# Matrix comparisons moved from the attention heads into the prologues

## The chip, the cores and the metric

The kernel runs on one core of one Trainium2 chip. Its engines are named as in the profile: PE (TensorE, matrix products), PEld (loading the weights of a product), DVE (VectorE), ACT (ScalarE), POOL (GpSimd) and SP (SyncE, which issues all of this kernel's transfers from one queue, in order). The metric is the device time of one execution in microseconds, the median of several runs.

## The reference

Two attention layers and two Fourier layers alternate, each with a layer norm in front and a residual sum behind; sequence 2048, width 640, 32 heads of 20, a sliding window of 256. All data are float32.

```python
def _A_ref(x, wqkv, wo):
    qkv = transpose((x @ wqkv).reshape(B, S, 3, H, Dh), 2, 0, 3, 1, 4)
    q, k, v = qkv[0], qkv[1], qkv[2]
    scores = jnp.einsum("bhqd,bhkd->bhqk", q, k) * (Dh ** -0.5)
    mask = (idx[:, None] - idx[None, :] >= 0) & (idx[:, None] - idx[None, :] < W)
    p = _softmax(jnp.where(mask[None, None], scores, -1e9), axis=-1)
    o = jnp.einsum("bhqk,bhkd->bhqd", p, v)
    return transpose(o, 0, 2, 1, 3).reshape(B, S, D) @ wo

def _B_ref(x, dft_seq_re, dft_seq_im, dft_hid_re, dft_hid_im):
    a = jnp.einsum("bsd,ed->bse", x, dft_hid_re)
    b = jnp.einsum("bsd,ed->bse", x, dft_hid_im)
    return jnp.einsum("ts,bse->bte", dft_seq_re, a) - jnp.einsum("ts,bse->bte", dft_seq_im, b)

x = x + _A_ref(_layernorm(x), A_wqkv, A_wo)
x = x + _B_ref(_layernorm(x), ...)
x = x + _A_ref(_layernorm(x), A_wqkv, A_wo)
x = x + _B_ref(_layernorm(x), ...)
```

The Fourier matrices are inputs like any other. The kernel computes the Fourier layers in a folded form that holds only if these matrices have the symmetries of a Fourier transform, and it tests that on the chip: this is what the "comparisons" or "checks" are. If a test fails, a general version of the whole network runs behind.

## The kernel before

**The layers.** Each attention layer has a prologue (`before_heads`), the heads (`heads`) and an end (`after_heads`); the Fourier layers follow (`fourier`). The program is written out in order: each engine executes its instructions in the order in which the Python code emits them, and waits for semaphores where data or buffers are not ready. In the heads small planners choose PSUM banks and post work to later steps (`post`, `tick`, `job`), but this too is settled when the program is built.

**The prologue.** It normalizes 16 tiles of 128 rows (`prep`: load, statistics on DVE, a power on POOL at L310, the normalization on DVE at L315, transposes on PE at L362, splitting into high and low parts on ACT at L243 and DVE at L249). Between these stand 16 value tiles (`value(t)`, t from 0 to 15, 30 matrix products each at L256) and, for each group of four tiles, two pieces of queries and keys (`pieces`, `piece`). A value tile fills two PSUM banks out of three (role "v": 5, 6, 7); ACT evicts the first (L478) and DVE the second (L480). After each second tile SP stores the pair to DRAM (`v_d<-pt`, L482). `packed` loads queries and keys back in the arrangement that the heads use (`kp<-qk_d`, `qp<-qk_d`, L639).

**The heads.** 128 steps in each attention, one 128-row block of a quad of heads each. Per step: four score products (L676) with a mask addition and row maximum on DVE each (L681), two pairs of transposed score products (L704), their exponentials on ACT (L714), the window's corners cleared on POOL (L720, L724), and the products with the values (L739). Beside them runs the projection of the remaining queries and keys (L274); its results pass through ACT (L589) and POOL (L597, L228), and its weights come as chunks that are split on ACT (L236) and DVE (L228, `wc<-x,wc`, two parts a chunk).

**A check.** `check(buf)` loads a block of four or eight parts of a matrix that should be equal or opposite (L1490, 214 or 228 KB, `rr<-kr` or the like), subtracts or adds the first part from or to the others (L1497, one or two instructions; on POOL in the attentions), squares and sums the result (L1501 on ACT, which also reads the sum). After each eighth check DVE adds up eight sums (L1506). There are 180 checks. In the prologue `check()` inside `before_heads` takes one of five small buffers in turn (`ou` and `rr`), and `check_step` holds a check's arithmetic back until two more have been begun, so a check's POOL and ACT instructions stand three checks behind its transfer in program order. In the heads `check_in_heads` issues a check at certain steps, `IN_HEADS` times over the first `CHECKED` = 81 steps (every six or seven steps), into the next `rr` buffer, with its three parts posted 6, 7 and 9 slots later. The Fourier layers take 14 buffers and work off the rest.

Before the change the first attention makes 16 checks in its prologue (6 in the pieces, 10 beside value tiles 4 to 13) and 12 in its heads; the second makes 22 (8 in the pieces, 14 beside value tiles 0 to 13) and 12. That is 62 of the 180.

Of the kernel before, what the change touches and what calls it, by code (L numbers as in the profile page):

```python
# [50 lines left out]
PRODUCTS = [(n, c) for n in ("ce", "co", "so", "se") for c in range(3)]  # L51
SIGMA, WIDE = 513, 57
SCALED, MARGIN = 2.0 ** 40, 2.0 ** 12
IN_HEADS, CHECKED = 12, 81

CHUNKS = ((0, 16, 0, 8), (0, 16, 8, 16), (16, 24, 0, 16), (24, 32, 0, 16), (0, 32, 16, 20))

# [16 lines left out]
class Net:  # L74
    def __init__(self, nc, tc, ctx, a, ok=None):
        self.nc, self.tc, self.a = nc, tc, a
        self.general = ok is None
        const = ctx.enter_context(tc.tile_pool(name="const", bufs=1))
        self.ln = ctx.enter_context(tc.tile_pool(name="ln", bufs=5))
        self.slots = ctx.enter_context(tc.tile_pool(name="slots", bufs=1))  # L80
        psum = ctx.enter_context(tc.tile_pool(name="psum", bufs=1, space=PSUM))
        self.work = ctx.enter_context(tc.tile_pool(name="work", bufs=2))
        dram = ctx.enter_context(tc.tile_pool(name="dram", bufs=1, space=DRAM))

        self.banks = psum.tile([P, 8, 512], F32, name="banks")

        def fixed(name, cols, dt):
            return const.tile([P, cols], dt, name=name)

        self.ident = fixed("ident", P, F32)  # L90
        nc.sync.dma_start(self.ident, a["ident"])
        self.flip = fixed("flip", P, F32)
        nc.sync.dma_start(self.flip, a["flip"])
        self.mask = fixed("mask", 384, BF16)
        self.ones = const.tile([1, 128], F32, name="ones")
        nc.vector.memset(self.ones, 1.0)
        self.half = fixed("half", 1, F32)
        nc.vector.memset(self.half, -0.5)
        self.big = [None] * 4
        self.qp, self.kp = [None] * 2, [None] * 2  # L100

        self.qk = dram.tile([2, 2 * D, S], F32, name="qk_d")
        self.vd = dram.tile([NQ, P, NB, 96], F32, name="v_d")
        self.od = dram.tile([H, 32, S], F32, name="o_d")
        self.rd = dram.tile([NSB, H, 512], F32, name="r_d")
        self.xs = [dram.tile([S, D], F32, name=f"x_d{i}") for i in range(3)]
        self.turn = {}
        self.xn = {}
        self.first = True
        self.slot = None  # L110
        self.posted = {}
        self.lanes = {n: deque() for n in ("act", "dve", "pool")}
        self.heavy = []
        self.left = 0
        self.tmp = None
        self.held = []
        self.bank_of = {}
        self.seen = fixed("seen", 2, F32)
        self.checks = deque() if self.general else deque(self.all_checks())
        self.stages = deque()  # L120
        self.n_checks = 0
        if not self.general:
            self.ok = ok
            self.ring = fixed("ring", 16, F32)
            self.part = fixed("part", len(self.checks) // 8 + 1, F32)
            self.norms = fixed("norms", 4, F32)
# [283 lines left out]
    def before_heads(self, xsrc):  # L410
        nc, a = self.nc, self.a
        self.proj = self.project()
        first = self.first
        vst = [t.rearrange("p (q t c) -> p q t c", t=2, c=96) for t in self.pt[:2]]
        for v in self.pt[:2]:
            (nc.vector if first else nc.gpsimd).memset(v, 1.0)
        for t in range(6):
            self.prep_load(xsrc, t)
            if first and 2 < t < 5:
                self.load_chunk(t - 3)  # L420
        if first:
            mask = self.raw()[:, :384]
            nc.sync.dma_start(mask, a["mask"])
        self.prep_stats(0)
        self.prep_stats(1)
        self.prep_norm(0)
        state = [0, 6]
        here = self.ou + self.rr
        wv = self.wv

        def check():
            here.append(here.pop(0))
            self.check_step(here[0][:, :8 * WIDE])

        def prep():
            r = state[0]
            if state[1] < r + 5:
                self.prep_load(xsrc, state[1])
                state[1] += 1
            self.prep_stats(r + 2)  # L440
            self.prep_norm(r + 1)
            if r == 10 or r == 11:
                self.prep_norm(r + 2)
            if r == 11:
                self.prep_stats(14)
                self.prep_stats(15)
                self.prep_norm(14)
            if r == 12:
                self.prep_norm(15)
            self.prep_turn(r)  # L450
            state[0] += 1

        def pieces(sb):
            for c in range(2):
                if sb == 0:
                    prep()
                self.piece(c, sb, "q")
                if c or sb > 1 or not first:
                    check()
                if sb and state[0] < 4 * sb + 8:  # L460
                    prep()

        def value(t):
            v, xt = vst[t // 2 % 2], self.xnt(t // 4)
            rs = slice((t % 4) * P, (t % 4 + 1) * P)
            ps = []
            for hf in range(2):
                p = self.bank("v", 320)
                cs = slice(hf * 320, (hf + 1) * 320)
                self.all3(p, [((xt[:, 0, k, rs], xt[:, 1, k, rs]), (wv[k][0][:, cs], wv[k][1][:, cs]))  # L470
                              for k in range(KC)])
                ps.append(p)
            prep()
            for hf in range(2):
                dst = v[:, 4 * hf:4 * hf + 4, t % 2, 0:84].rearrange("p q (h c) -> p q h c", c=21)[:, :, :, 1:21]
                src = ps[hf].rearrange("p (q h c) -> p q h c", q=4, h=4)
                if hf == 0:
                    nc.scalar.activation(dst, src, AF.Copy)  # L478
                else:
                    nc.vector.tensor_copy(dst, src)  # L480
            if t % 2:
                nc.sync.dma_start(self.vd[:, :, t - 1:t + 1, :].rearrange("q p t c -> p q (t c)"),  # L482
                                  v.rearrange("p q t c -> p q (t c)"))
            if 3 < t < 14 or t < 4 and not first:
                check()
            elif t > 13:
                for _ in range(t - 13):
                    self.check_step()

        def values(sb):  # L490
            for i in range(4):
                value(4 * sb + i)

        def packed(sb):
            for f in self.pack(0, sb):
                f()

        self.split_w(4)
        prep()
        self.split_w(6)  # L500
        prep()
        self.split_w(3 * KC)
        for t in range(4):
            if t in (1, 2):
                self.cut_chunk(t - 1)
            value(t)
        if first:
            nc.gpsimd.tensor_copy(self.mask, mask)
        while state[1] < NB:
            self.prep_load(xsrc, state[1])  # L510
            state[1] += 1
        pieces(0)
        pieces(1)
        self.take_qk("kp", 0)
        self.ones_rows(0)
        packed(0)
        packed(1)
        values(1)
        pieces(2)
        self.load_chunk(2)  # L520
        packed(2)
        values(2)
        pieces(3)
        self.cut_chunk(2)
        self.load_chunk(3)
        packed(3)
        values(3)
        while self.stages:
            self.check_step()
        self.pt += [self.slot_tile(f"pt{i}", 3 * 512, F32) for i in (2, 3)]  # L530
        for name in ("kp", "qp"):
            self.take_qk(name, 1)
        self.ones_rows(1)
# [1178 lines left out]
```

## Time and profile before

| what | value |
|---|---|
| median of three runs | 1366.66 us (1366.66, 1367.58, 1358.52) |
| the profiled execution's own time | 1368.62 us |
| its span on the core | 1366.9 us |
| first prologue | about 0 to 124 us |
| first attention's heads and end | about 124 to 600 us |
| first Fourier layer | about 600 to 688 us |
| second prologue | about 688 to 797 us |
| second attention's heads and end | about 797 to 1260 us |
| second Fourier layer | about 1260 to 1367 us |

The table's stages are read from when each line first and last runs. A profile row begins with the line of the kernel (L681), the engine, the operation and the tiles written and read; busy time adds up an engine's instructions, and the idle time of a group is the time that its engine stood still just before it, with the event that ended it. The clock column is the share of TensorE's full clock. Busy time on PE is modelled from starts of matrix products, so a PE that is called busy is not one at its peak.

### The profile page before, as it was taken

How to read it: one execution, taken by the hardware profiler on the slowest of the kernel's cores; microseconds unless marked ns; L12 is line 12 of the kernel's file. 1: busy time of each engine (PE TensorE's matmuls, PEld its weight loads, DVE VectorE, ACT ScalarE, POOL GpSimd, SP SyncE). 2: the span in 40 equal slices, each digit the busy share in tenths (PEclk: the TensorE clock that was granted, in tenths of full speed). 3: DMA queues.
4: the chain of work that ended last, by engine and by line, in shares of the span. 5: the costliest groups of instructions: out<-in, count | busy, mean ns of one | idle time of the engine just before them, and what ended most of it. 6: DMA issues, size and time to landing. Idle time of an engine off the chain costs nothing.

```text
span 1366.9 us, 37415 instructions
## 1 busy us (share of the span) xinstructions
PE 1293.2 (95%) x13350; PEld 995.8 (73%) x13350; DVE 973.2 (71%) x3117; ACT 761.4 (56%) x1651; POOL 729.3 (53%) x1508
## 2 busy tenths in 40 slices
PE   6999999999998999999999999999999988989996
PEld 6899777777776777753689997777777767778344
DVE  6723788888887774776866247888888877657674
ACT  3232378776876565446323225777777755744463
POOL 4221677776777673310334237787777875733043
PEclk9999999999999999999999999999999999999999
DMA  5675567776668864527536755676777688571565
GB/s 196 209 221 175 183 196 202 211 199 188 205 208 239 225 201 141 164 77 225 193 110 203 228 163 184 195 201 197 213 201 223 211 245 198 169 213 56 169 209 205
DMA packets 174297, 261.49 MB, mean 191 GB/s; under 512 B 36306, under 2 KB 85586, under 8 KB 174100
## 3 DMA queue, kind: packets, MB, share of 16 engines
q1 hardware_dynamic: 174100, 259.00, 62.8%
q8 instruction: 108, 1.77, 0.6%
q14 instruction: 89, 0.73, 0.2%
HBM read 175.42 MB, written 82.31 MB: 189 GB/s over the span
## 4 chain that ended last, share of the span: by engine, by line
PE 40%; DMA 3%; DVE 3%; issue 2%; ACT 2%; POOL 1%; SPq 1%; ACTq 0%; POOLq 0%; DVEq 0%
PE banks L274 10%; PE banks L256 8%; PE banks L739 5%; PE banks L704 4%; PE banks L676 4%; PE banks L1301 3%; PE banks L1409 3%; DMA big<-x_d 1%; PE banks L1425 1%; DVE banks L681 1%; ACT pt L714 1%; DMA qp<-qk_d 1%; DMA qp<-mt 1%; PE banks L362 1%; POOL rs L1156 0%
## 5 line engine op out<-in xcount | busy, mean ns | idle before, releaser
L681 DVE CUSTOM_DVE_ANT_0 banks<-banks,mask 128x384 f32<-128x384 f32 (+2 forms) x1024 | 527.0, 556 | 115.4 <-PE banks L676 97.3
L714 ACT ACTIVATE pt<-banks 128x768 f32<-128x768 f32 (+2 forms) x512 | 394.9, 773 | 163.3 <-PE banks L704 80.7
L720 POOL TENSOR_SCALAR_AFFINE_SELECT pt<-pt 128x256 f32<-128x256 f32 x512 | 219.7, 429 | 198.4 <-ACT pt L714 173.4
L274 PE MATMUL banks<-big,wc 64*128 64x512 f32 x1920 | 272.9, 394 | 0.4 <-DVE pt L480 0.4
L704 PE MATMUL banks<-qp,kp 61*128 61x384 f32 (+2 forms) x1024 | 209.8, 380 | 25.3 <-DVE mc L681 19.7
L676 PE MATMUL banks<-kp,qp 60*128 60x384 f32 (+2 forms) x1024 | 209.3, 352 | 8.5 <-DVE mc L681 5.1
L739 PE MATMUL banks<-pt,vq 128*32 128x128 f32 x5760 | 211.4, 278 | 0.9 <-ACT pt L714 0.8
L274 PEld LDWEIGHTS banks<-big,wc 64*128 64x128 f32 x1920 | 187.7, 186 | 22.0 <-ACT x L589 1.5
L724 POOL TENSOR_SCALAR_AFFINE_SELECT pt<-pt 128x256 f32<-128x256 f32 x448 | 186.5, 416 | 0.0
L739 PEld LDWEIGHTS banks<-pt,vq 128*32 128x32 f32 x5760 | 142.4, 110 | 49.3 <-issue 35.7
L704 PEld LDWEIGHTS banks<-qp,kp 61*128 61x128 f32 x1024 | 108.1, 185 | 88.9 <-DVE mc L681 66.5
L676 PEld LDWEIGHTS banks<-kp,qp 60*128 60x128 f32 x1024 | 124.5, 187 | 34.7 <-DVE mc L681 20.5
L681 DVE DVE_READ_ACCUMULATOR2_ANT mc<- 128x1 f32 x1024 | 143.7, 140 | 0.0
L748 ACT ACTIVATE ou<-banks 128x128 f32<-128x128 f32 (+2 forms) x288 | 73.7, 268 | 62.0 <-PE banks L739 55.3
L256 PE MATMUL banks<-qp,big 128*128 128x320 f32 x576 | 99.6, 318 | 1.0 <-POOL qp L382 1.0
L228 POOL TENSOR_TENSOR c<-x,c 128x256 fp32r<-128x256 f32 x128 | 94.3, 744 | 0.0
L256 PEld LDWEIGHTS banks<-qp,big 128*128 128x128 f32 x576 | 89.5, 194 | 1.6 <-POOL qp L382 1.4
L256 PE MATMUL banks<-qp,kp 128*128 128x320 f32 x384 | 82.2, 346 | 6.5 <-ACT big L1121 4.2
L274 PE MATMUL banks<-big,big 64*128 64x320 f32 x912 | 81.3, 314 | 0.2 <-ACT mt L692 0.2
L256 PEld LDWEIGHTS banks<-qp,kp 128*128 128x128 f32 x384 | 61.0, 188 | 19.9 <-ACT big L1121 6.2
L274 PEld LDWEIGHTS banks<-big,big 64*128 64x128 f32 x912 | 74.1, 191 | 0.4 <-ACT mt L692 0.4
L1497 POOL TENSOR_TENSOR rr<-rr 128x171 f32<-128x171 f32 (+3 forms) x76 | 48.5, 648 | 47.2 <-DMA rr<-hr 17.9
(170 smaller groups left out, 1787.2 us busy)
## 6 DMA issues: line engine op xcount, KB each, us to landing
qk_d<-c SPq DMA_DIRECT2D x80, 512.0 KB
kp<-qk_d SPq DMA_DIRECT2D x384, 80.0 KB
qp<-qk_d SPq DMA_DIRECT2D x384, 80.0 KB
o_d<-ou SPq DMA_DIRECT2D x64, 256.0 KB
v_d<-pt SPq DMA_DIRECT2D x16, 768.0 KB
vq<-v_d SPq DMA_DIRECT2D x64, 192.0 KB
kp<-ki SPq DMA_DIRECT2D x44, 228.0 KB
big<-x SPq DMA_DIRECT2D x26, 320.0 KB
```

What stands on the lines that cost most here:

```text
L228: eng.tensor_tensor(out=lo[..., c], in0=src[..., c], in1=hi[..., c].bitcast(F32), op=OP.subtract)
L256: self.nc.tensor.matmul(p, x, y, start=n == 0, stop=n == last)
L274: self.nc.tensor.matmul(ps[a], x[r], y[r], start=half + i == 0, stop=half == 1 and i == n - 1, skip_group_check=True)
L676: nc.tensor.matmul(p, qp[quad % 2][b:b + 60, z, qb * P:(qb + 1) * P], kp[quad % 2][b:b + 60, z, k0 * P:(qb + 1) * P], start=True, stop=True)
L681: nc.vector.tensor_tensor_reduce(out=p, in0=p, in1=self.mask[:, 384 - n * P:], scale=1.0, scalar=NEG, op0=OP.add, op1=OP.max, accum_out=mc ...
L704: nc.tensor.matmul(self.banks[:, banks[e], :n * P], kp[quad % 2][b:b + 61, z, kb * P:(kb + 1) * P], qp[quad % 2][b:b + 61, z, kb * P:(kb + ...
L714: nc.scalar.activation(pt[quad, kb][:, 2 * z:2 * z + 2, :n * P], self.banks[:, b0:b1 + 1, :n * P], AF.Exp, scale=SCALE)
L720: nc.gpsimd.affine_select(out=t[:, :, 0:P], in_=t[:, :, 0:P], pattern=[[0, 2], [1, P]], compare_op=OP.is_ge, fill=0.0, base=0, channel_mul ...
L724: nc.gpsimd.affine_select(out=t[:, :, 256:384], in_=t[:, :, 256:384], pattern=[[0, 2], [-1, P]], compare_op=OP.is_gt, fill=0.0, base=0, ch ...
L739: nc.tensor.matmul(self.banks[32 * h:32 * h + 32, bank, :P], vq[:, 96 * (kb % 4) + 21 * h:96 * (kb % 4) + 21 * h + 32], t[:, h, (qb - kb) ...
L748: nc.scalar.activation(ou[:, dst], self.banks[:, bank, src], AF.Copy)
L1497: eng.tensor_tensor(out=t[:, lo:hi], in0=t[:, lo:hi], in1=base.broadcast_to([P, hi - lo, w]), op=op)
```

## The change

No check is made in the heads any more (`IN_HEADS` is 0). In the prologues every value tile from 0 to 13 makes a check, in the first attention too, where tiles 0 to 3 had none; from tile 4 on it makes two. So the first prologue makes 30 checks and the second 32, 62 together as before; the first Fourier layer begins with the 31st check and not with the 29th. The counter `checked`, which the heads used to set, now gets a start value. The order of checks, their arithmetic and the two drains beside tiles 14 and 15 are the same. Since one line is added above it and another further below, line numbers of the changed kernel are 1 or 2 higher.

```diff
-IN_HEADS, CHECKED = 12, 81
+IN_HEADS, CHECKED = 0, 81
...
         self.n_checks = 0
+        self.checked = 0
...
-            if 3 < t < 14 or t < 4 and not first:
-                check()
+            if t < 14:
+                for _ in range(1 + (3 < t)):
+                    check()
             elif t > 13:
                 for _ in range(t - 13):
                     self.check_step()
```

## The prediction

> **What bounds the kernel now.** I read the page first, then the busy time by stage, then what the matrix engine (PE) waited for in the stages that the change touches, then one stretch of the timeline in which it stood still. The page's first lines:
>
> ```profile
> span 1366.9 us, 37415 instructions
> ...
> PE 1293.2 (95%) x13350; PEld 995.8 (73%) x13350; DVE 973.2 (71%) x3117; ACT 761.4 (56%) x1651; POOL 729.3 (53%) x1508
> ```
>
> Busy time of each engine in single stretches: two of the first prologue, one of the first attention's heads, then the same two stages of the second attention (columns: stretch, its length, the five busy times with instruction counts, clock, DMA share, GB/s):
>
> ```profile
> core 0: us, PE busy (x) PEld busy (x) DVE busy (x) ACT busy (x) POOL busy (x), PEclk, DMA share, GB/s
> ...
> 60.00:80.00 20.00, 20.00 (x128) 18.79 (x127) 11.81 (x30) 6.62 (x22) 5.82 (x9) 1.00 0.71 220
> ...
> 100.00:120.00 20.00, 20.00 (x125) 19.06 (x124) 3.83 (x6) 5.68 (x18) 3.88 (x8) 1.00 0.82 235
> ...
> 200.00:300.00 100.00, 98.93 (x1410) 75.67 (x1406) 85.26 (x317) 75.25 (x150) 73.74 (x169) 1.00 0.74 210
> ...
> 750.00:770.00 20.00, 20.00 (x132) 19.33 (x131) 5.11 (x12) 6.65 (x21) 5.73 (x11) 1.00 0.85 260
> ...
> 850.00:950.00 100.00, 98.20 (x1411) 75.35 (x1405) 82.17 (x312) 74.77 (x147) 75.85 (x177) 1.00 0.69 198
> ```
>
> In the prologues PE never stops, and ScalarE (ACT) and GpSimd (POOL) are idle two thirds of the time; the DMA engines are the fullest resource beside PE. In the heads PE has only about 1 to 2 us of idle in 100, while VectorE (DVE), ACT and POOL are all busy three quarters of the time. So taking work off ACT and POOL in the heads can win only what PE loses there. PE's waits, from 160 to 400 us (heads) and from 690 to 800 us (second prologue); columns are total, times, longest:
>
> ```profile
> PE banks L676 <- DVE mc L681: 3.5, 1, 3.5
> PE banks L704 <- DVE mc L681: 2.6, 7, 0.6
> ```
>
> ```profile
> PE banks L362 <- DVE big L249: 1.1, 1, 1.1
> ```
>
> One single wait of 3.5 us is more than all others of that stretch of the heads. The timeline around it (columns: start, duration, engine, line, what; in brackets the idle time before it):
>
> ```profile
> 299.50 0.97 POOL L1497 TENSOR_TENSOR rr<-rr 128x399 f32<-128x399 f32 x1
> ...
> 302.53 0.56 ACT L1501 ACTIVATE rr<-rr 128x399 f32<-128x399 f32 x1
> ...
> 302.95 0.23 ACT L1501 ACTIVATION_READ_ACCUMULATOR rr<-rr 128x1 f32 x1
> ...
> 303.21 0.16 DVE L1506 TENSOR_REDUCE part<-ring 128x1 f32<-128x8 f32 x1 [0.16 <-ACT rr L1501]
> ...
> 304.28 4.80 DVE L228 TENSOR_TENSOR wc<-x,wc 128x384 fp32r<-128x384 f32 x1
> ...
> 304.52 0.42 POOL L720 TENSOR_SCALAR_AFFINE_SELECT pt<-pt 128x256 f32<-128x256 f32 x1
> ...
> 307.94 0.74 POOL L228 TENSOR_TENSOR c<-x,c 128x256 fp32r<-128x256 f32 x1
> ...
> 309.41 0.33 PE L676 MATMUL banks<-kp,qp 60*128 60x128 f32 x2 [3.51 <-DVE mc L681]
> ```
>
> A check's three parts stand right ahead of it: the comparison on POOL, the square on ACT, the sum on DVE. Then DVE's subtraction of a weight chunk (two operands in SBUF) lasts 4.80 us, for as long as POOL runs without a pause, and ends just after POOL's last operation of that run does (307.94 + 0.74 = 308.68, against 309.08). The mask additions behind it on DVE, and so PE's score matmuls, come late.
>
> What that cost is read by comparing weight chunks. The same subtraction for the chunk before and after, and for the same three chunks of the second attention (with POOL's neighbours of the middle one):
>
> ```profile
> 261.30 0.75 DVE L228 TENSOR_TENSOR wc<-x,wc 128x384 fp32r<-128x384 f32 x1
> ```
>
> ```profile
> 352.84 0.81 DVE L228 TENSOR_TENSOR wc<-x,wc 128x384 fp32r<-128x384 f32 x1
> ```
>
> ```profile
> 935.41 0.75 DVE L228 TENSOR_TENSOR wc<-x,wc 128x384 fp32r<-128x384 f32 x1
> ```
>
> ```profile
> 979.08 0.73 POOL L228 TENSOR_TENSOR c<-x,c 128x256 fp32r<-128x256 f32 x1
> ...
> 979.32 0.91 DVE L228 TENSOR_TENSOR wc<-x,wc 128x384 fp32r<-128x384 f32 x1
> ...
> 979.77 0.73 POOL L720 TENSOR_SCALAR_AFFINE_SELECT pt<-pt 128x256 f32<-128x256 f32 x1
> ```
>
> ```profile
> 1022.18 0.82 DVE L228 TENSOR_TENSOR wc<-x,wc 128x384 fp32r<-128x384 f32 x1
> ```
>
> From 261.30 to 304.28 it is 42.98 us, from 304.28 to 352.84 it is 48.56, and in the second attention 43.91 and 42.86. The stall cost 48.56 - 42.86 = 5.7 us, or 5.6 against the stretch before it.
>
> [...]
>
> **The change, part by part.** *1. What leaves the heads.* On POOL, at the stalled place of the first attention, before:
>
> ```order
> L720 AFFINE_SELECT pt_1247<-pt_1247 128x2x128
> L724 AFFINE_SELECT pt_1247<-pt_1247 128x2x128
> L1497 TENSOR_TENSOR rr_107<-rr_107 128x399
> L720 AFFINE_SELECT pt_102<-pt_102 128x2x128
> L724 AFFINE_SELECT pt_102<-pt_102 128x2x128
> L597 CAST c<-x 128x512
> ```
>
> and now:
>
> ```order
> L722 AFFINE_SELECT pt_1293<-pt_1293 128x2x128
> L726 AFFINE_SELECT pt_1293<-pt_1293 128x2x128
> L722 AFFINE_SELECT pt_102<-pt_102 128x2x128
> L726 AFFINE_SELECT pt_102<-pt_102 128x2x128
> L599 CAST c<-x 128x512
> ```
>
> The comparison is gone; ACT's square, DVE's sum and the transfer of 228 KB on SP's queue go too. PE's rows stand in the same order before and after. The sizes, from the groups of 160 to 400 us and, last, 840 to 1080 us (count, then busy us and mean ns, then idle):
>
> ```profile
> L1497 POOL TENSOR_TENSOR rr<-rr 128x399 f32<-128x399 f32 (+2 forms) x14 | 11.6, 826 | 0.0
> ...
> L1501 ACT ACTIVATE rr<-rr 128x399 f32<-128x399 f32 (+1 forms) x12 | 6.3, 524 | 0.0
> ```
>
> ```profile
> L1497 POOL TENSOR_TENSOR rr<-rr 128x171 f32<-128x171 f32 (+1 forms) x24 | 13.7, 570 | 1.0 <-DMA rr<-ki 1.0
> ```
>
> Who waited for the comparison in the first heads (us, times):
>
> ```profile
>   ACT pt L714: 0.8, 1
>   PEld banks L739: 0.2, 1
> ```
>
> 11.6 + 13.7 = 25.3 us leave POOL, and 2 x 6.3 = 12.6 us (with the read of each sum some more) leave ACT. On PE's path lie: the stall, -5.6 if it goes; and the rest, bounded by nothing on one side and by all of ACT's 12.6 us on the other. The nearest rows are the direct waits, 0.8 + 0.2 in one attention and 1.0 for a transfer in the other: I take -1.5 for both. Term 1 is therefore -7.1. I expect the stall to go, because all three checks' parts that made POOL and DVE late are gone there; what may still be late next is the same subtraction, if POOL again finds no pause.
>
> *2. What enters the prologues.* SP's queue in the second prologue, the third group of value tiles (8 to 11), before:
>
> ```order
> L1490 DMA ou_8916<-kr 128x456
> L482 DMA v_d<-pt_8914 128x8x192
> L1490 DMA ou_8917<-kr 128x456
> L1490 DMA rr_8918<-kr 128x456
> L482 DMA v_d<-pt_8915 128x8x192
> L1490 DMA rr_8919<-kr 128x456
> ```
>
> and now:
>
> ```order
> L1492 DMA rr_8929<-kr 128x456
> L1492 DMA ou_8925<-ki 128x456
> L483 DMA v_d<-pt_8923 128x8x192
> L1492 DMA ou_8926<-ki 128x456
> L1492 DMA rr_8927<-ki 128x456
> L1492 DMA rr_8928<-ki 128x456
> L1492 DMA rr_8929<-ki 128x456
> L483 DMA v_d<-pt_8924 128x8x192
> L1492 DMA ou_8925<-ki 128x456
> L1492 DMA ou_8926<-ki 128x456
> ```
>
> Two transfers stand where one stood, five buffers as before, so a buffer comes round after two and a half tiles, not five, and a square follows its transfer by one and a half tiles, not three. First attention: 14 checks more (four beside tiles 0 to 3, ten beside 4 to 13), 12 fewer in its heads; second: 10 more and 12 fewer. Compute costs nothing: per tile one comparison (about 1.1 us of POOL) and one square with its sum (302.53 to 303.18, about 0.7 us of ACT), while in the 20 us stretches above, some 4.5 tiles, POOL has over 14 us free and ACT over 13, under a PE that is busy for all 20. If that cover failed, 24 x 0.7 = 17 us of ACT would show.
>
> The queue is tighter. One odd tile of the second prologue, from the timeline (SPq rows are issues):
>
> ```profile
> 764.12 0.51 SPq L482 DMA_DIRECT2D v_d<-pt  x1
> ...
> 764.72 0.53 SPq L1490 DMA_DIRECT2D ou<-kr  x1
> ...
> 765.69 0.44 ACT L478 ACTIVATE pt<-banks 128x320 f32<-128x320 f32 x1 [3.44 <-PE banks L256]
> ...
> 770.09 0.44 ACT L478 ACTIVATE pt<-banks 128x320 f32<-128x320 f32 x1 [3.44 <-PE banks L256]
> ...
> 770.75 1.10 POOL L1497 TENSOR_TENSOR ou<-ou 128x171 f32<-128x171 f32 x2 [1.46 <-DMA ou<-kr]
> ```
>
> A tile takes 770.09 - 765.69 = 4.40 us. The transfer issued at 764.72 landed at 770.75, 6.03 us later. In the new order its square stands between those two evictions on ACT: comparison done at 771.85, square at 772.6, eviction at 773.0 instead of 770.5. The value banks are three, two per tile, so PE wants that bank back one tile after the eviction could start, at 774.5. Reserve 1.5 us. One more transfer ahead in the queue is
>
> ```profile
> rr<-kr SPq DMA_DIRECT2D x30, 228.0 KB
> ```
>
> 228 KB at the 260 GB/s of 750 to 770 us, 0.9 us: still inside. I take +0.5, with 0 and the slower rival's price as ends. Queued behind SP's waits are the value stores, the loads of kp and qp and the next weight chunk, all wanted a tile or more later.
>
> *3. Meeting DVE in the prologue.* In the first tiles POOL now works beside DVE's normalization:
>
> ```profile
> 7.71 0.61 DVE L315 TENSOR_SCALAR big<-big,mv,rs 128x640 f32<-128x640 f32 x1
> ...
> 9.02 3.30 POOL L382 TENSOR_TENSOR qp<-kp,qp 128x640 fp32r<-128x640 f32 x2 [0.29 <-ACT qp L379]
> ...
> 9.46 1.45 DVE L315 TENSOR_SCALAR big<-big,mv,rs 128x640 f32<-128x640 f32 x1
> ```
>
> Beside POOL it took 1.45 instead of 0.61 us. Eight such meetings per attention would be 7 us of DVE, which has 8 of 20 us free at 60 to 80 us and works a tile ahead: 0. [...]
>
> *4.* Two checks fewer are left to the first Fourier layer in the cheap form: two more comparisons on DVE, under matmuls, 0.
>
> **Sum.** The profiled execution took 1368.6 us (span 1366.9 and 1.7 around it): 1368.6 - 7.1 + 0.5 = 1362.0. It is 2.0 above the median of the runs (1366.66; the others 1367.58 and 1358.52), so against the median 1360. I say 1361. The run of 1358.52 is about what a run without the stall would give.
>
> **Rivals.** *Nothing won (0.26).* [...]
>
> *More won (0.12).* The runs that set the median had two such stalls: 1366.7 - 2 x 5.6 - 1.5 = 1354. The trace shows one.
>
> *Slower (0.10).* The prologue's transfers land too late: with the DMA share at 0.85 and one more 228 KB in 4.4 us (52 GB/s on 260, so 0.85 x 1.2 = 1.02) the queue fills, the ACT square waits, the eviction behind it waits, and PE has no bank. It decides when a transfer takes over 6.0 + 1.5 = 7.5 us to land; at 9.5 us each of the odd tiles 5 to 13, five per attention, loses 2 us: 10 x 2 = 20, and 1361 + 20 = 1381. Against: loaded stretches alternate with pieces in which the share is lower (0.71 at 60 to 80 us), so the queue drains.
>
> **How the numbers follow.** Forecast 0.52, its own range 1356 to 1366. The range 1353 to 1371 takes in the two rivals without loss and the milder half of the slower one, and leaves out the rest. 1% is 13.7 us, about what a measurement of this kernel can tell from no change: below 1353 only part of the third case, 0.06; above 1380 half of the slower one and a little for causes not seen, 0.06; between, 0.88.
>
> **What would show it.** Right: in the changed profile every L228 subtraction of a weight chunk on DVE under 1.3 us, chunk distances of 43 to 44 us in both attentions, PE busy 20 of 20 us in the prologues, the DMA share there near 0.9 to 1.0. Wrong: a 4 us subtraction again; PE idle in the value tiles behind evictions on ACT; or the heads' chunk distances shorter by more than 1 us each, which would mean that the checks cost more than their waits show.

## The result and the profile after

The changed kernel takes 1373.01 us (median of 15 runs, 1368.34 to 1376.68), the kernel before 1363.65 (15 runs beside it, 1355.41 to 1370.85). The ratio is 1.0062, with a 95% interval of 1.0042 to 1.0082: slower by some 8.5 us, by less than the 1% that the prediction took as its bound. The prediction said 1361, a gain, in a range of 1353 to 1371. The ratios here and below leave out five executions that ran far longer as a whole (one of 1548.86 us at a mean clock of 0.753, four of over 3000 us).

The profiled execution of the changed kernel is its fastest one, 1368.34 us, and that of before was among the slower ones, 1368.62. Their spans tell nothing, therefore; the stages do. The page's first lines, after:

```profile
span 1366.6 us, 37474 instructions
...
PE 1288.9 (94%) x13350; PEld 995.1 (73%) x13350; DVE 970.7 (71%) x3119; ACT 764.5 (56%) x1651; POOL 732.6 (54%) x1506
```

Where a prologue ends is read from the first score product of each attention. PE's timeline around these, before and after (start, duration):

```profile
123.07 0.33 PE L676 MATMUL banks<-kp,qp 60*128 60x128 f32 x2
...
796.61 0.33 PE L676 MATMUL banks<-kp,qp 60*128 60x128 f32 x2
```

```profile
132.72 0.33 PE L678 MATMUL banks<-kp,qp 60*128 60x128 f32 x2
...
806.83 0.33 PE L678 MATMUL banks<-kp,qp 60*128 60x128 f32 x2
```

The first prologue is 132.72 - 123.07 = 9.65 us longer. The second began at 687.8 before and at 688.0 after (first product on its normalized rows, read from the trace), so it grew by 10.0. From the first to the last transposed score product (L704 before) the first attention's heads took 371.9 us before and 363.9 after, the second's 371.4 and 365.4. So this pair of executions has +19.6 in the prologues and -14.0 in the heads; the other -6 lies behind the heads, in stretches that the change leaves as they were. Part of that is scatter: in the profiles below, the two heads together took 731.9 to 740.3 us in three further executions of before (743.3 in this one), and 730.5 to 735.3 in four other kernels without checks there (729.3 in this one); the stretch behind the second heads took 160 to 165 us in all these profiles, for a reason that was not found. What the pair does show is a loss in the prologues against a gain in the heads.

Busy time by stretch, after (columns as in the prediction: stretch, length, PE, PEld, DVE, ACT, POOL, clock, DMA share, GB/s), and behind it a stretch of the second prologue before:

```profile
60.00:80.00 20.00, 15.07 (x92) 14.70 (x91) 8.98 (x26) 5.14 (x18) 8.46 (x14) 0.84 0.65 189
...
100.00:120.00 20.00, 20.00 (x122) 18.81 (x121) 3.75 (x7) 8.37 (x27) 9.66 (x12) 1.00 0.82 261
200.00:300.00 100.00, 99.29 (x1441) 76.50 (x1437) 84.61 (x317) 72.92 (x140) 72.09 (x167) 1.00 0.68 196
730.00:750.00 20.00, 15.69 (x106) 15.40 (x105) 11.85 (x33) 6.20 (x19) 9.00 (x17) 0.90 0.77 221
```

```profile
730.00:750.00 20.00, 20.00 (x136) 19.32 (x135) 13.02 (x35) 6.66 (x20) 8.31 (x14) 1.00 0.72 197
```

PE, which was busy for 20.00 us at 60 to 80 us, is now busy for 15.07, and the clock was 0.84 where it had been 1.00. The same at 730 to 750. ACT and POOL are still idle more than half of that time. PE's waits in the two prologues, after (total, times, longest):

```profile
PE banks L257 <- ACT pt L479: 6.6, 2, 4.9
```

```profile
PE banks L257 <- ACT pt L479: 7.2, 3, 4.3
```

Before there was no wait for the eviction of a value tile (L478 there) at all. The longest, from the timeline after (SPq rows are issues; in brackets the idle time before a row; here and below, rows of other instructions in between are left out):

```profile
56.80 2.41 SPq L641 DMA_DIRECT2D kp<-qk_d  x6
59.25 2.38 SPq L641 DMA_DIRECT2D qp<-qk_d  x6
61.69 3.00 SPq L641 DMA_DIRECT2D kp<-qk_d  x6
64.85 2.72 SPq L641 DMA_DIRECT2D qp<-qk_d  x6
68.09 0.84 SPq L1492 DMA_DIRECT2D rr<-hr  x2
...
73.07 1.55 POOL L1499 TENSOR_TENSOR rr<-rr 128x321 f32<-128x321 f32 x2 [5.04 <-DMA rr<-hr]
73.89 0.47 ACT L1503 ACTIVATE rr<-rr 128x321 f32<-128x321 f32 x1 [5.27 <-POOL rr L1499]
...
75.00 0.44 ACT L479 ACTIVATE pt<-banks 128x320 f32<-128x320 f32 x1
75.49 2.77 PE L257 MATMUL banks<-qp,big 128*128 128x320 f32 x9 [4.93 <-ACT pt L479]
```

Read from the bottom: PE waits 4.93 us for the eviction at 75.00; that stands behind a check's square on ACT, which waited 5.27 us for the comparison; that waited 5.04 us on POOL for the check's transfer; and the transfer was issued at 68.09 because SP first issued 24 loads of queries and keys, from 56.80 to 67.57. In program order the check's transfer stands right behind these loads. The same place before:

```profile
67.28 0.37 SPq L1490 DMA_DIRECT2D rr<-hr  x1
...
68.91 0.43 ACT L478 ACTIVATE pt<-banks 128x320 f32<-128x320 f32 x1
...
71.60 0.80 POOL L1497 TENSOR_TENSOR rr<-rr 128x321 f32<-128x321 f32 x1 [3.35 <-DMA rr<-hr]
73.74 0.45 ACT L478 ACTIVATE pt<-banks 128x320 f32<-128x320 f32 x1
74.06 0.48 ACT L1501 ACTIVATE rr<-rr 128x321 f32<-128x321 f32 x1
```

The transfer came no earlier, at 67.28, and POOL waited for it too, 3.35 us. But its square stood three tiles behind it, after the evictions at 68.91 and 73.74, and nobody waited. Now three checks are one and a half tiles, and the square stands ahead of the eviction that had its turn at 68.91 and now gets it at 75.00. The same columns as above, after, in short stretches:

```profile
70.00:76.00 6.00, 1.07 (x6) 0.81 (x6) 1.03 (x3) 1.99 (x7) 1.55 (x2) 0.81 0.95 299
76.00:80.00 4.00, 4.00 (x17) 3.96 (x16) 0.33 (x2) 0.57 (x2) 3.48 (x7) 0.50 0.14 51
740.00:748.00 8.00, 4.03 (x29) 3.76 (x27) 2.11 (x7) 1.94 (x7) 3.69 (x7) 0.88 0.87 231
748.00:752.00 4.00, 3.66 (x14) 3.66 (x15) 1.12 (x3) 1.44 (x5) 2.72 (x6) 0.50 0.59 224
128.00:140.00 12.00, 9.90 (x82) 8.17 (x82) 3.96 (x19) 3.84 (x12) 3.73 (x4) 1.00 0.64 196
```

While PE stands still (70 to 76 us, and part of 740 to 748) ACT, POOL and DVE do little either; the DMA engines are at 0.95 and 0.87, working off the loads and the checks' transfers behind them. Behind each of the two long idles, 4.93 and 4.31 us, PE runs at half clock (0.50 from 76 to 80 and from 748 to 752 us; the nine products at 75.49 took 2.77 us, the same nine at 68.10 took 1.58); behind the short one, 1.71 us at 130 us, it doesn't (1.00 from 128 to 140). Four microseconds at 0.50 cost another 2. So the first prologue's 9.65 is 6.6 of waiting and at least 2 of half clock, the second's 10.0 is 7.2 of waiting and again some 2 of half clock.

In the heads, the ten subtractions of a weight chunk from 160 to 400 us (busy us, mean ns), before and after:

```profile
L228 DVE TENSOR_TENSOR wc<-x,wc 128x384 fp32r<-128x384 f32 (+1 forms) x10 | 11.6, 1160 | 0.0
```

```profile
L229 DVE TENSOR_TENSOR wc<-x,wc 128x384 fp32r<-128x384 f32 (+1 forms) x10 | 7.4, 745 | 0.0
```

The blocked one is gone, as forecast.

### The profile page after: what moved, and what is told of

Read it like the earlier page. It is cut to its first block, busy times and chain, and to the rows that moved or that the text cites. A ratio compares the mean times of both kernels' runs of the same rounds, so it can differ in the third digit from the quotient of the medians.

```text
span 1366.6 us, 37474 instructions
## 1 busy us (share of the span) xinstructions
PE 1288.9 (94%) x13350; PEld 995.1 (73%) x13350; DVE 970.7 (71%) x3119; ACT 764.5 (56%) x1651; POOL 732.6 (54%) x1506
## 4 chain that ended last, share of the span: by engine, by line
PE 36%; DMA 6%; DVE 4%; issue 3%; ACT 2%; POOL 2%; SPq 1%; POOLq 0%; ACTq 0%; DVEq 0%
PE banks L275 9%; PE banks L741 5%; PE banks L257 4%; PE banks L706 4%; PE banks L678 4%; PE banks L1411 3%; PE banks L1303 3%; DMA kp<-qk_d 1%; PE banks L1427 1%; DMA big<-x_d 1%; DVE banks L683 1%; DMA qp<-qk_d 1%; DMA qk_d<-c 1%; DMA rr<-kr 1%; POOL rs L1158 0%
## 5 line engine op out<-in xcount | busy, mean ns | idle before, releaser
L275 PE MATMUL banks<-big,big 64*128 64x320 f32 x912 | 78.5, 307 | 0.2 <-ACT mt L694 0.2
L1499 POOL TENSOR_TENSOR rr<-rr 128x171 f32<-128x171 f32 (+5 forms) x61 | 36.8, 628 | 63.1 <-DMA rr<-kr 28.9
```

The source lines that it names most:

```text
L275: self.nc.tensor.matmul(ps[a], x[r], y[r], start=half + i == 0, stop=half == 1 and i == n - 1, skip_group_check=True)
```

## The experiments

**The theory** was this: the heads win about what was forecast or more, and the prologues lose more than that, because a check's square now stands so close behind its transfer that the transfers behind SP's block of 24 (or 12) loads come too late. **The rivals:** the heads won nothing, and the lower time there is scatter; or the prologues lose by the added volume and work itself, wherever it stands. In the expectations a letter A is the theory held at that time, other letters are its rivals. The ratios are to the kernel before, run beside each on the same chip; they are turned into microseconds at 1364.

### The heads alone

From the kernel before. No check is made in the heads, and 24 checks, as many as were made there, are left out of the kernel altogether, so it does less work than the kernel before.

```diff
-IN_HEADS, CHECKED = 12, 81
+IN_HEADS, CHECKED = 0, 81
...
-        self.checks = deque() if self.general else deque(self.all_checks())
+        self.checks = deque() if self.general else deque(c for n, c in enumerate(self.all_checks()) if not 19 <= n < 31 and not 100 <= n < 112)
...
+        self.checked = 0
```

> The kernel before without its 24 checks in the heads; they are left out altogether (156 of 180 are made), the prologues are as before. Theory A (checks in the heads cost PE the blocked subtraction and a little more, about 7 us in each attention, as the two profiles' heads of 371.9 and 371.4 us against 363.9 and 365.4 us say): 10 to 14 us below the kernel before, both heads near 365 us. Rival (the heads were bound by PE and won nothing; the shorter heads were chance): within 3 us of the kernel before.

Measured: 1355.21 us, ratio 0.9939 (0.9914 to 0.9965), so -8.3 us with -11.7 to -4.8. The heads did win; the first rival falls. It is somewhat less than the theory's figure, and close to the forecast's -7.1.

### The prologues alone

From the changed kernel: the prologues as changed and the heads' checks kept, by making 24 checks a second time.

```diff
-IN_HEADS, CHECKED = 0, 81
+IN_HEADS, CHECKED = 12, 81
...
+        if not self.general:
+            todo = list(self.checks)
+            self.checks = deque(todo[:28] + [todo[27]] * 14 + todo[28:112] + [todo[111]] * 10 + todo[112:])
```

> The changed prologues with the heads as before; 24 checks are made twice, so that both places have theirs. Theory A (the prologues lose about 10 us each to evictions that wait behind late transfers): 16 to 22 us above the kernel before, prologues of 132 and 118 us against 123 and 109. Rival (the prologues' loss in the profile was chance or comes from the empty heads): within 4 us of the kernel before.

Measured: 1370.83 to 1377.88 us in four runs, ratio 1.0113 (1.006 to 1.0165), so +15.4 us with +8.2 to +22.5. By the medians alone, 1375.15 of the four against 1363.72 beside them, it would be +11.4, so the size is known only roughly. A profile of the same kernel:

> The changed prologues with the heads as before, 24 checks made twice; one more profile. Theory A: PE waits near 5 us once in each prologue behind an eviction of value tiles on ACT (tiles 4 and 5), prologues of about 132 and 118 us. Rival: prologues of 123 and 109 us.

It took 1377.03 us in one run. PE's waits in its two prologues, for the eviction of value tiles:

```profile
PE banks L260 <- ACT pt L482: 4.3, 2, 3.5
```

```profile
PE banks L260 <- ACT pt L482: 6.4, 3, 4.4
```

It is the wait of the changed kernel, and it comes without any change to the heads. The prologues, measured as above, are 127.9 and 117.8 us long, against 123.1 and 108.8 in the first profile of before: the second lost what was expected, the first only half of it. The two parts add up within their intervals: -8.3 + 15.4 = +7.1, against +8.5 measured for the whole.

### Same work, loads handed out in smaller portions

From the changed kernel: the loads of queries and keys are put in a list and issued six behind each value tile, instead of 24 or 12 at once.

```diff
+        loads = deque()
...
+                for _ in range(min(6, len(loads))):
+                    loads.popleft()()
...
-            for f in self.pack(0, sb):
-                f()
+            loads.extend(self.pack(0, sb))
```

> The changed kernel, but the loads of queries and keys that SP issues 24 and 12 at a time are handed out six behind each value tile. Theory A (SP is busy for some 11 us with 24 loads, the transfers of tile 4's checks come out behind them, and squares, evictions and PE wait): the waits of PE for evictions at 70 and 744 us go, prologues 3 to 10 us shorter each, 6 to 18 us below the changed kernel. Rival B (it is the volume: twice the transfers, comparisons and squares beside a tile, in whatever order): within 4 us of the changed kernel, the waits stay.

Measured: 1361.37 us, ratio 0.9987 (0.9954 to 1.0019), so -1.8 where the changed kernel has +8.5. All 62 checks are still made in the prologues. PE's waits in the second prologue:

```profile
PE banks L363 <- DVE big L250: 3.0, 2, 1.9
PE banks L363 <- DVE x L316: 2.2, 1, 2.2
PE banks L257 <- ACT pt L479: 0.3, 1, 0.3
```

The waits for the eviction went from 7.2 to 0.3. Some of it turned up as waits for DVE's share of the splitting (L250), 3.0 instead of 1.1, and in the first prologue 3.5 instead of 1.1. So with the block of loads cut up the distance of one and a half tiles does no such harm, but that is not yet a gain. The run takes away both the late issue and the bytes that stand ahead of the check in the DMA engines; these two weren't told apart.

### Same order, more distance

From the changed kernel: three more buffers (the heads' value buffers `vq`, which the prologue leaves idle), and a check's arithmetic six checks behind its transfer, not three. With two checks per tile these are three tiles, as before the change. SP's order is untouched.

```diff
+        self.hold = 5
...
-        here = self.ou + self.rr
+        here = self.ou + self.rr + self.vq
...
-                for _ in range(t - 13):
+                for _ in range(3):
                     self.check_step()
...
-        if self.stages and (len(self.stages) > 2 or buf is None):
+        if self.stages and (len(self.stages) > self.hold or buf is None):
```

> The changed kernel with eight check buffers instead of five (the three value buffers that the heads use later) and a check's arithmetic held back by six checks instead of three, which is three value tiles as before the change; SP's order is otherwise the same. Theory A (it is the halved distance between a transfer and its square that lets a late transfer stop ACT): prologues within 2 us of 123 and 109 us, 12 to 20 us below the changed kernel and 5 to 12 below the kernel before. Rival B (volume): within 4 us of the changed kernel.

Measured: 1356.82 us, ratio 0.9958 (0.993 to 0.9987), so -5.7 us: faster than the kernel before and than the changed one. The same place as above in its timeline, and its busy time by stretch:

```profile
67.56 0.37 SPq L1493 DMA_DIRECT2D vq<-hr  x1
...
73.87 0.80 POOL L1500 TENSOR_TENSOR vq<-vq 128x321 f32<-128x321 f32 x1 [2.84 <-DMA vq<-hr]
74.48 0.45 ACT L480 ACTIVATE pt<-banks 128x320 f32<-128x320 f32 x1
74.80 0.48 ACT L1504 ACTIVATE vq<-vq 128x321 f32<-128x321 f32 x1
```

```profile
60.00:80.00 20.00, 20.00 (x128) 18.74 (x127) 12.99 (x32) 9.33 (x32) 10.99 (x18) 1.00 0.79 235
730.00:750.00 20.00, 19.40 (x126) 18.20 (x126) 11.72 (x31) 9.72 (x31) 14.44 (x27) 1.00 0.76 232
```

The transfer is issued as late as ever, at 67.56, POOL waits for it as before the change, and the eviction at 74.48 passes ahead of the square at 74.80. PE is busy for 20.00 and 19.40 of 20 us again, with more bytes moved (235 GB/s against 189) and more ACT and POOL work in the stretch. The second rival falls: neither the volume nor the work was the price.

### A smaller distance

How much distance does it take? From the changed kernel again: one more buffer, and four checks, which are two tiles.

```diff
+        self.hold = 3
...
-        here = self.ou + self.rr
+        here = self.ou + self.rr + self.vq[:1]
...
-                for _ in range(t - 13):
+                for _ in range(2):
...
-        if self.stages and (len(self.stages) > 2 or buf is None):
+        if self.stages and (len(self.stages) > self.hold or buf is None):
```

> The changed kernel with six check buffers and a hold of four checks, which is two value tiles: between the change (one and a half) and the deep version (three). Theory A (the distance between transfer and square must cover SP's 11 us of loads and the landing, some 15 us; two tiles are 8.8): waits for evictions remain but shorter by about half a tile, 2 us each; 1362 to 1370. Rival (any distance over one and a half tiles is enough, or the two extra buffers matter by themselves): as the deep version, 1354 to 1360.

Measured: 1356.45 us, ratio 0.9946 (0.992 to 0.9973), so -7.4. The expectation of a time between the two was wrong: two tiles do as well as three. The one wait for an eviction that is left, in the second prologue:

```profile
PE banks L258 <- ACT pt L480: 1.2, 1, 1.2
```

The step from one and a half to two tiles puts one more eviction ahead of a square, and that is enough. Distance and number of buffers were changed together, and no run tells them apart; but at the place shown above the transfer was issued right behind the block of loads with five buffers (68.09) as with eight (67.56), so it was not a missing buffer that made it late there.

### What the heads paid for

The prediction had put most of the heads' gain down to one blocked subtraction. It is not in every execution. The kernel before, profiled again three times:

> The kernel before, unchanged, profiled once more. If the blocked subtraction in the first attention's heads comes in most executions: again one subtraction of a weight chunk on DVE over 4 us, and 48 us between two chunks. If it is a rare accident: all of them under 1.3 us.

> The kernel before, one more profile. If the blocked subtraction is what sets the slower of its times: a blocked one goes with a time near 1367, none with a time near 1357.

> As the run before it, a fourth profile of the kernel before.

They took 1354.2, 1358.6 and 1363.48 us. The ten subtractions from 160 to 400 us in each, in this order:

```profile
L228 DVE TENSOR_TENSOR wc<-x,wc 128x384 fp32r<-128x384 f32 (+1 forms) x10 | 8.0, 797 | 0.0
```

```profile
L228 DVE TENSOR_TENSOR wc<-x,wc 128x384 fp32r<-128x384 f32 (+1 forms) x10 | 7.6, 756 | 0.0
```

```profile
L228 DVE TENSOR_TENSOR wc<-x,wc 128x384 fp32r<-128x384 f32 (+1 forms) x10 | 7.4, 742 | 0.0
```

None has the 4.80 us of the first profile. And the time of before is not set by it alone: the third of these took 1363.48 without it. What differs there is mostly a stretch late in the heads: counted by the transposed score products, the steps 96 to 112 of an attention took from 55.5 to 61.5 us in the traces of all these kernels, with checks or without, for a reason that was not found.

Two runs then gave the heads half of a check each, on top of the kernel without the 24 checks: only the transfers of 228 KB (nothing is computed on them), or only the arithmetic, a comparison on POOL and a square on ACT at the old steps, on buffers that are not loaded (they are set to zero once at the start), and without the sum on DVE. Both leave out 24 checks, as the run with the heads alone does.

```diff
+    def load_in_heads(self, buf):
+
+        self.nc.sync.dma_start(buf, self.a["kr" if self.first else "ki"][0, 1])
```

> The heads' checks reduced to their transfers: 12 loads of 228 KB in each attention's heads at the old steps, into the same buffers, with no comparison, square or sum; 24 checks are left out, prologues as before. Theory A (the arithmetic on POOL, ACT and DVE is what the heads lost by): within 3 us of the kernel with no checks in the heads, some 8 below the kernel before. Rival (the loads on SP's queue and the DMA engines cost it): within 3 us of the kernel before.

```diff
+    def work_in_heads(self, buf):
...
+        cut = 8 if self.first else 4
+        self.post(6, lambda: differ(1, cut, OP.subtract))
+        if cut < 8:
+            self.post(7, lambda: differ(cut, 8, OP.add))
+        self.post(9, square)
```

> The heads' checks reduced to their arithmetic: the comparison on POOL and the square on ACT at the old steps, on whatever the buffers hold, without a load and without the sum of eight on DVE; 24 checks are left out, prologues as before. Theory A: within 3 us of the kernel before, with a blocked subtraction in the heads as there. Rival (loads): some 8 us below the kernel before. In between, with no blocked subtraction: the DVE sum behind the square takes part in the stall.

Transfers alone: 1359.54 us, ratio 0.9977 (0.9943 to 1.001), or -3.1 us with -7.8 to +1.4: the transfers may cost up to all of the gain or little of it, and the 8 us that were expected did not come. Arithmetic alone: median 1351.53, ratio 0.9917 (0.9887 to 0.9947), or -11.3 us, as good as no checks at all. That the arithmetic is what costs was the expectation in both, and it was wrong for the median. But the execution of it that was profiled took 1363.58, against 1350.12 to 1354.39 for its other four, and it has the blocked subtraction, with POOL's instruction that it met and POOL's next one:

```profile
305.73 0.73 POOL L230 TENSOR_TENSOR c<-x,c 128x256 fp32r<-128x256 f32 x1
306.19 4.78 DVE L230 TENSOR_TENSOR wc<-x,wc 128x384 fp32r<-128x384 f32 x1
306.41 0.40 POOL L724 TENSOR_SCALAR_AFFINE_SELECT pt<-pt 128x256 f32<-128x256 f32 x1
```

So the stall came here without a check's transfer; and when it strikes it costs what the prediction thought: from this chunk's subtraction to the next one's (354.61) it is 48.4 us, against 43.0 for the chunk before (263.19 to 306.19). Why that execution is some 10 us above the others, and not 5, is not known. The stall showed in three of the seven profiles of kernels with POOL comparisons in the heads and this subtraction on DVE (one of four of before; one of two of the prologues alone, 4.78 us at 310.30; arithmetic alone), and in none of the six without comparisons there.

A last run took the subtraction from DVE, in the kernel before, with all of its checks:

```diff
-                self.cut_job("dve", ("w", c), w[:, 0, ks], w[:, 1, ks], raw[:, ks])
+                self.cut_job("pool", ("w", c), w[:, 0, ks], w[:, 1, ks], raw[:, ks])
```

> The kernel before, with the weight chunks' subtraction in the heads moved from DVE to POOL; checks in the heads as before. Theory A (what the heads lose to the checks is the subtraction on DVE that POOL blocks): no blocked subtraction, the stretch of eight steps from step 48 back at 21.4 us, and 3 to 8 us below the kernel before. Rival (the checks cost the heads through POOL's and ACT's own time): no faster than the kernel before, or slower, since POOL gets 13 us more in each attention.

Measured: 1362.07 us, ratio 0.9978 (0.9952 to 1.0005). Without a subtraction on DVE there is nothing to block, and the gain is 3 us at best guess, not separable from none. But POOL now makes the subtractions as well, so the run shows what the stall and this added work come to together, not the stall alone. What the stall, the transfers and the arithmetic each have in the heads' 8 us stays open.

## Why the prediction was wrong

**The step that failed** is the second of the change, "What enters the prologues", and in it the sentence "One more transfer ahead in the queue is ... 228 KB at the 260 GB/s of 750 to 770 us, 0.9 us: still inside. I take +0.5 ...". It measured +15.4 (+8.2 to +22.5). The reasoning to the wait was whole: the new distance of one and a half tiles, the square on ACT ahead of the eviction, the three value banks, the reserve of 1.5 us. But the reserve was worked out at an odd tile in the third group, where what stands ahead of the transfer on SP is a value store of half a microsecond. The tile that decides is the one behind `packed`, where 24 loads stand ahead. In the changed kernel SP issued the check's transfer at 68.09, behind the last of them (67.57), in program order. The prediction's list of what waits on SP had the loads as waiting for the checks, and not the checks as waiting for the loads. The row that could have warned stood in the trace before: POOL's 3.35 us of idle behind `rr<-hr` at 71.60, at the time a wait that cost nothing because three tiles stood behind it.

**The slower rival** had the right chain ("the ACT square waits, the eviction behind it waits, and PE has no bank"), and the wrong place and cause. It wanted a loss of 2 us at five odd tiles per attention, from DMA engines that one more transfer per tile overfills throughout. They were full where PE stood still (0.95, 0.87), but behind the block of loads only, at two or three places per prologue, 4.93 and 4.31 us at the worst; over 60 to 80 us their share was 0.65, less than before (0.71), and with the same volume and more distance the only wait for an eviction left was one of 0.6 us. Its 1381 is not far from the 1371 to 1378 of the prologues alone, but its 0.10 rested on a queue that drains, which it does everywhere but there, and the range took in only its milder half. With that term at its measured size the sum would have been 1368.6 - 7.1 + 15.4 = 1376.9, which is 2 above the median of the basis, so 1375 for 1373 measured (or 1371 with the 11.4 of the medians). That this comes so near is in part luck, because the first term is less sure than it looks.

**The heads, -7.1**, were right in sign and size (-8.3, with -11.7 to -4.8), by a less certain way than was said, so the near match of the size is luck in part. The 5.6 of the stall belong to executions that have it, one of the four profiled. The prediction itself showed the second attention's subtraction meeting a POOL operation on either side at 0.91 us (979.32), without a stall, and should have drawn the consequence for the term: a price times a share of executions, and a larger one for the rest than the -1.5 that was taken from direct waits. *Nothing won* is refuted by the run with the heads alone. The stall showed again in two more profiles, at 4.78 us in both (prologues alone, arithmetic alone), far longer than any one POOL instruction beside it (0.40 to 0.74 us each in the two cases below). *More won* has its 1354 near what the heads alone gave, 1355.21, but not for its reason; no profile shows two stalls.

**DVE's normalization beside POOL** and the first Fourier layer, taken at 0: no wait of the changed prologues names them that was not there before, and with the longer distance the same meetings cost nothing that can be seen.

**What was to show it:** the subtractions below 1.3 us came true, and so did the chunk distances of 43 to 44 us (43.1 to 43.4 in the changed kernel). "PE busy 20 of 20 us in the prologues" failed, and the DMA share, expected near 0.9 to 1.0, was 0.65 to 0.82 in the stretches of 20 us shown above; "PE idle in the value tiles behind evictions on ACT" is what happened, word for word.

## What to carry to other kernels

When work on an in-order engine is held back by a number of items, and more items are put into each step, the distance in time shrinks by the same factor (here the waits for evictions in the second prologue were 7.2 us at one and a half tiles, 1.2 at two): keep it in steps, with buffers to match, before anything else is costed. The reserve of a transfer is worked out at the place where its queue has the most ahead of it, not at a typical one, and a wait that costs nothing today is the first place to look for it. A stall that one profile shows is priced by how often it strikes, so profile the kernel before more than once.

## What the runs showed of the hardware

DVE's subtraction of a weight chunk (`wc<-x,wc`, 128x384) took 4.78 to 4.80 us once in each of three profiles, against 0.76 to 0.77 for each of the five in the first attention's heads of the changed kernel. In two of the three, the first of before and the arithmetic alone, it began 0.44 and 0.46 us after a subtraction on POOL had, ran beside an unbroken run of short POOL instructions (0.40 to 0.74 us each), and ended 0.40 and 0.43 us after the last of them. Nearly the same meeting in the second of the later profiles of before took 0.69:

```profile
304.61 0.73 POOL L228 TENSOR_TENSOR c<-x,c 128x256 fp32r<-128x256 f32 x1
305.06 0.69 DVE L228 TENSOR_TENSOR wc<-x,wc 128x384 fp32r<-128x384 f32 x1
305.29 0.73 POOL L720 TENSOR_SCALAR_AFFINE_SELECT pt<-pt 128x256 f32<-128x256 f32 x1
```

Here DVE began 0.45 us after POOL's subtraction and ended 0.41 us after it did (304.61 + 0.73 = 305.34), and it was POOL's next selection that took longer, 0.73 us where it took 0.40 and 0.42 in the two stalls. The moment of meeting alone doesn't decide which of the two takes longer, or hundredths of a microsecond do. In the changed kernel, without comparisons on POOL in the heads, the two engines met in the first attention at the same point in every chunk: POOL's subtraction began 0.73 to 0.74 us ahead of DVE's at each of the five larger subtractions. With them, in the first profile of before, it began 0.18, 0.70, 0.75, 0.44 (the stall) and 0.70 us ahead. That may be why taking the comparisons out of the heads ends the stall; no run tested it.

PE's clock in the changed kernel went to 0.50 behind idles of 4.93 and 4.31 us and stayed at 1.00 behind 1.71. In the same trace it was 0.52 from 688 to 691 us, right behind an idle of 2.18 us, and in the kernel before 0.59 over the same stretch, behind one of 2.17 us. So in these traces idles of little more than 2 us, too, had a low clock behind them.

SP took 10.8 us to issue 24 loads of 80 KB, 0.45 us each (56.80 to 67.57), and the next transfer in program order, a check's, was issued at 68.09. The DMA engines were busy too just then (0.95 from 70 to 76 us), and how much of the check's delay that made was not told apart.
